# Another order of up and down products in the 256-column passes of the second mixture of experts

## The chip, the cores and the metric

The kernel runs on one core of a Trainium2 chip. The metric is device time in microseconds (us) of one execution; lower is better.

## What is computed

Three stages follow each other: an attention masked by clusters (2 x 8 heads, 768 positions, head size 64), a first mixture of experts with a maximum over three products, and the second mixture of experts, in which the change lies. Cut to that stage:

```
x: 1536 x 512, w_gate: 512 x 8, w1: 8 x 512 x 1024, w2: 8 x 1024 x 512
P = exp(x @ w_gate - max)
8 times: P /= row sums; P /= column sums; P *= N / E
for e in range(8):
    h = max(x @ w1[e], 0)
    out += P[:, e:e+1] * (h @ w2[e])
```

## The kernel before, in words

All products are float32: each operand is split into a high and a low part, and `three` (lines 705 to 709) issues three matmuls for one product of 128 rows.

The second mixture works in 32 **units**, n = 0 to 31: one expert and one pair of 128-row slices of its 1024 hidden columns. Each unit has two **passes** over the tokens (`PASSES`): a **wide** one (i = 0) of 512 columns and a **narrow** one (i = 1) of 256 columns. Tokens are halved, so that a Strassen-like scheme of seven products stands for eight.

`up_products` yields after each of its seven products; an **up block** is six matmuls of 512 or 256 columns. In the order of the code they are, with the accumulator bank they write: U1 (x), U2 (y), U3 (x again, added), U4 (y again, added), U5 (z), U6 (w), U7 (z again, added). What reads them in between:

- after U1, ScalarE copies bank x to `a` (L1062). U3 adds to bank x, so it waits for that copy.
- after U2, VectorE adds y and `a` into `u2` (L1065). U4 adds to bank y, so it waits for that add.
- after U3, a rectifier (L1045 on ScalarE, L1046 on VectorE) makes the first hidden tile, h11; after U4, VectorE adds y and `a` into `u3` (L1071).
- U5, U6 and U7 are followed by one VectorE add or subtraction each (c22 L1074, c21 L1078, c12 L1082) and a rectifier each. U7 waits for the read of bank z by c22.

`down` yields after each **down block** (D): six matmuls of 512 columns into one of four banks `l`, then one VectorE instruction that scales and accumulates into `acc` (L1106; L1101 for the first expert, L1104 besides for its last pair). Down blocks work on the pass before: a narrow pass runs the eight down blocks D1 to D8 of its unit's wide pass, and a wide pass runs the four of the previous unit's narrow pass.

The order in which a pass issues up and down blocks is a string in the table `WAYS` (L1116), `u` for up and `d` for down, and nothing else reorders it: each engine runs its instructions in program order.

```
WAYS = {(0, 0): "uuuu", (0, 1): "uudddudddudd", 0: "uuduuduudud", 1: "uuddudududududd"}
```

Between the blocks, counted by up blocks, the loop also issues the weight conversions of the next unit (ScalarE, L863 and L873, GpSimd, L864 and L874), the fetch of further weights (SyncE, after the fourth up block of a narrow pass), and in units 1 and 2 the steps of the gate (the repeated normalisation of P): after the second, fourth and sixth up block of a pass a small matmul `cs` (L1018) on TensorE and a chain of eight small VectorE instructions (L1010 to L1025), which ends in `prob` (L1015) and which the next `cs` waits for.

Of the kernel before, what the change touches and what calls it, by code (L numbers as in the profile page):

```python
# [137 lines left out]
def moe_kernel(ctx: ExitStack, tc: tile.TileContext, qk, nat, cen, wt, w123, wout, wgate, w1, w2, out):  # L138
# [974 lines left out]
    gate = gates()  # L1113
    later = iter(())

    WAYS = {(0, 0): "uuuu", (0, 1): "uudddudddudd", 0: "uuduuduudud", 1: "uuddudududududd"}  # L1116
    for n in range(len(seq)):
        for i in range(2):
            if i == 0:
# [8 lines left out]
            k = 0  # L1128
            for step in WAYS[(0, i) if n == 0 else i]:
                if step == "d":  # L1130
# [69 lines left out]
```

## Time and profile before

| | |
|---|---|
| three runs, us | 1484.22, 1485.67, 1486.05 (median 1485.67) |
| profiled execution, us | 1484.61, of which span 1482.8 |
| TensorE busy | 1446.4 us, 98% of the span |
| VectorE, ScalarE, GpSimd busy | 964.1, 542.1 and 701.8 us (65%, 37%, 47%) |
| second mixture, narrow passes of units 1 to 31 | from 524.28 us to the end |

The page has the busy times, the span in 40 slices, the chain of work that ended last, and the costliest groups. A matmul's end in it is modelled, and matmuls overlap, so the distance between the starts of neighbouring matmuls, rather than the printed duration, tells how long one keeps TensorE. In the second mixture the sequence repeats with a period of 31.00 us per unit from unit 3 on.

### The profile page before, as it was taken

The numbers are of one execution on the slowest core, as the hardware profiler recorded it, in microseconds if no ns is written. First come the engines' busy times: TensorE is split into PE (matmuls) and PEld (weight loads), VectorE is DVE, ScalarE is ACT, GpSimd is POOL, SyncE is SP. The second block draws the span as 40 slices with busy tenths as digits, with TensorE's granted clock in tenths as the row PEclk, the third lists the DMA queues.
The fourth block names the chain that finished last, engine by engine and source line by source line (L and its number), as shares of the span: only waits on it lengthen the run. The fifth ranks groups of instructions, "written<-read, shape, count | busy, mean of one in ns | idle before, by whom it ended". The sixth has DMA issues, their size and how long they took to land.

```text
span 1482.8 us, 20473 instructions
## 1 busy us (share of the span) xinstructions
PE 1446.4 (98%) x7712; PEld 1247.1 (84%) x7712; DVE 964.1 (65%) x1686; ACT 542.1 (37%) x1159; POOL 701.8 (47%) x789
## 2 busy tenths in 40 slices
PE   5999998899999999999999999999999999999998
PEld 4999998788887888888888888888888888888887
DVE  5999888745555686765665655656556665566655
ACT  4888878422223522222222222222223222222221
POOL 5899998755654733343333333333333333333330
PEclk9999999999999999999999999999999999999999
DMA  6664631212121100111000110001100011000102
GB/s 176 174 162 130 154 82 47 69 43 71 54 64 42 56 29 29 30 46 39 29 29 29 44 43 29 29 30 43 43 29 29 29 44 43 29 29 29 44 15 86
DMA packets 32147, 83.44 MB, mean 56 GB/s; under 512 B 4560, under 2 KB 9904, under 8 KB 32048
## 3 DMA queue, kind: packets, MB, share of 16 engines
q1 hardware_dynamic: 32048, 82.13, 19.1%
q8 instruction: 60, 0.98, 0.3%
q14 instruction: 39, 0.32, 0.1%
HBM read 65.55 MB, written 3.19 MB: 46 GB/s over the span
## 4 chain that ended last, share of the span: by engine, by line
PE 84%; DVE 6%; POOL 6%; issue 1%; ACT 1%; DMA 1%; SPq 0%; POOLq 0%; ACTq 0%; DVEq 0%
PE l L707 11%; PE l L708 11%; PE l L709 11%; PE m L707 3%; PE m L709 3%; PE m L708 3%; PE z L709 3%; PE z L708 3%; PE z L707 3%; PE y L709 3%; PE x L709 3%; PE y L708 3%; PE x L708 3%; PE y L707 3%; PE x L707 3%; PE y L510 2%
## 5 line engine op out<-in xcount | busy, mean ns | idle before, releaser
L1106 DVE SCALAR_TENSOR_TENSOR acc<-l,prob,acc 128x512 f32<-128x512 f32 x336 | 251.6, 749 | 126.4 <-PE l L709 123.2
L707 PE MATMUL l<-w,h 128*128 128x512 f32 x768 | 302.2, 393 | 0.0
L708 PE MATMUL l<-w,h 128*128 128x512 f32 x768 | 301.1, 392 | 0.0
L709 PE MATMUL l<-w,h 128*128 128x512 f32 x768 | 298.8, 389 | 0.0
L1045 ACT ACTIVATE h<-c 128x512 fp32r<-128x512 f32 (+1 forms) x186 | 97.6, 525 | 368.8 <-DVE c L1074 190.6
L864 POOL TENSOR_TENSOR wop_t<-ts,wop_t 128x256 fp32r<-128x256 f32 x124 | 91.8, 751 | 245.3 <-ACT wop_t L863 245.3
L864 POOL TENSOR_TENSOR wop_b<-wraw,wop_b 128x256 fp32r<-128x256 f32 x97 | 79.3, 818 | 266.6 <-ACT wop_b L863 266.6
L1046 DVE SCALAR_TENSOR_TENSOR h<-c,h 128x512 fp32r<-128x512 f32 (+1 forms) x186 | 112.6, 605 | 110.0 <-ACT h L1045 110.0
L709 PEld LDWEIGHTS l<-w,h 128*128 128x128 f32 x768 | 144.3, 188 | 31.5
L707 PEld LDWEIGHTS l<-w,h 128*128 128x128 f32 x768 | 145.0, 189 | 24.5
L708 PEld LDWEIGHTS l<-w,h 128*128 128x128 f32 x768 | 145.0, 189 | 22.7
L874 POOL TENSOR_TENSOR w<-wraw,w 128x512 fp32r<-128x512 f32 x64 | 83.2, 1301 | 96.3 <-ACT w L873 96.3
L463 DVE TENSOR_SCALAR_CACHE_REDUCE e<-s 128x768 f32<-128x768 f32 x96 | 92.6, 964 | 17.8 <-PE s L452 17.1
L1045 ACT ACTIVATE h<-x 128x512 fp32r<-128x512 f32 (+1 forms) x62 | 30.4, 491 | 188.2 <-PE x L709 188.2
L471 ACT ACTIVATE e<-e,nm 128x768 f32<-128x768 f32 x96 | 90.0, 937 | 16.3 <-DVE e L463 15.8
L510 PE MATMUL y<-at,v 128*128 128x256 f32 x576 | 91.1, 293 | 3.2 <-DVE x L527 2.0
L510 PEld LDWEIGHTS y<-at,v 128*128 128x128 f32 x576 | 79.5, 192 | 6.2 <-POOL at L239 1.8
L707 PE MATMUL m<-x,mhi 128*128 128x512 f32 x216 | 84.0, 389 | 0.0
L708 PE MATMUL m<-x,mlo 128*128 128x512 f32 x216 | 84.0, 389 | 0.0
L709 PE MATMUL m<-x,mhi 128*128 128x512 f32 x216 | 84.0, 389 | 0.0
L709 PE MATMUL x<-x,wop_b 128*128 128x512 f32 (+1 forms) x248 | 83.3, 336 | 0.0
L709 PE MATMUL y<-s,wop_t 128*128 128x512 f32 (+1 forms) x248 | 83.3, 336 | 0.0
(203 smaller groups left out, 3304.7 us busy)
## 6 DMA issues: line engine op xcount, KB each, us to landing
wraw<-in_w SPq DMA_DIRECT2D x64, 512.0 KB
mraw<-in_w SPq DMA_DIRECT2D x18, 512.0 KB
nat<-in_nat SPq DMA_DIRECT2D x16, 384.0 KB
raw<-in_qk SPq DMA_DIRECT2D x16, 384.0 KB
natv<-in_nat SPq DMA_DIRECT2D x16, 192.0 KB
r<-row SPq DMA_DIRECT2D x16, 192.0 KB
mraw<-in_wout SPq DMA_DIRECT2D x8, 384.0 KB
out<-acc SPq DMA_DIRECT2D x12, 256.0 KB
```

The source lines that it names most:

```text
L463: lambda e: nc.vector.tensor_scalar(ex(), scores(), -SCALE, None, op0=ALU.mult, op1=ALU.min, accum_out=nm()),
L471: lambda e: nc.scalar.activation(ex(), ex(), AF.Exp, bias=nm(), scale=-1.0, accum_out=sm()[:, n]),
L510: nc.tensor.matmul(y(), v()[:, k], at()[:, l, :, k // 3, k % 3 * P : (k % 3 + 1) * P], start=n == 0, stop=n == 2 * NQ - 1)
L707: nc.tensor.matmul(ps, whi, xlo, start=first, stop=False, skip_group_check=more)
L708: nc.tensor.matmul(ps, wlo, xhi, start=False, stop=False, skip_group_check=more)
L709: nc.tensor.matmul(ps, whi, xhi, start=False, stop=last, skip_group_check=more)
L864: nc.gpsimd.tensor_sub(w[:, 1], src[key], f32(w[:, 0]))
L874: nc.gpsimd.tensor_sub(w[:, 1], raw[:, j], f32(w[:, 0]))
L1045: nc.scalar.activation(h[:, :, 0], z, AF.Relu)
L1046: nc.vector.scalar_tensor_tensor(h[:, :, 1], z, 0.0, f32(h[:, :, 0]), op0=ALU.max, op1=ALU.subtract)
L1106: nc.vector.scalar_tensor_tensor(acc[tt], l2, prob[:, tt, e : e + 1], acc[tt], op0=ALU.mult, op1=ALU.add)
```

## The change

One string of the table changes, that of the narrow pass of units 1 to 31: four up blocks, four down, one up, three down, two up, one down. The same seven up and eight down blocks are issued, with the same instructions behind each.

```diff
-    WAYS = {(0, 0): "uuuu", (0, 1): "uudddudddudd", 0: "uuduuduudud", 1: "uuddudududududd"}
+    WAYS = {(0, 0): "uuuu", (0, 1): "uudddudddudd", 0: "uuduuduudud", 1: "uuuudddduddduud"}
```

TensorE, narrow pass of unit 8, before: the first of the six matmuls of each block (`x8`, `y8` are the banks of U1 to U4, `l2` those of the down blocks; `[waits ...]` names the engines whose semaphores it waits for).

```order
L707 MATMUL x8_1_7963<-x2_0_5044,wop8_b11_7604 128x256 [waits PE_49]
...
L707 MATMUL y8_1_7964<-s2_0_5327,wop8_t2_7631 128x256
...
L707 MATMUL l2_8_1_0_0_7993<-w2_8_0_7787,h8_0_21_7931 128x512 [waits Activation_49,Pool_49]
...
L707 MATMUL l2_8_1_0_1_8001<-w2_8_0_7787,h8_0_21_7931 128x512
...
L707 MATMUL x8_1_7963<-x2_2_5234,wop8_b21_7662 128x256 [waits Activation_49]
...
L707 MATMUL l2_8_1_0_2_8021<-w2_8_0_7787,h8_0_21_7931 128x512 [waits DVE_49]
...
L707 MATMUL y8_1_7964<-s3_0_5328,wop8_t3_7708 128x256 [waits DVE_49]
...
L707 MATMUL l2_8_1_0_3_8041<-w2_8_0_7787,h8_0_21_7931 128x512
```

The same place now:

```order
L707 MATMUL x8_1_7963<-x2_0_5044,wop8_b11_7604 128x256 [waits PE_49]
...
L707 MATMUL y8_1_7964<-s2_0_5327,wop8_t2_7631 128x256
...
L707 MATMUL x8_1_7963<-x2_2_5234,wop8_b21_7662 128x256 [waits Activation_49]
...
L707 MATMUL y8_1_7964<-s3_0_5328,wop8_t3_7708 128x256 [waits DVE_49]
...
L707 MATMUL l2_8_1_0_0_8017<-w2_8_0_7787,h8_0_21_7931 128x512 [waits Pool_49]
...
L707 MATMUL l2_8_1_0_1_8025<-w2_8_0_7787,h8_0_21_7931 128x512
...
L707 MATMUL l2_8_1_0_2_8033<-w2_8_0_7787,h8_0_21_7931 128x512
...
L707 MATMUL l2_8_1_0_3_8041<-w2_8_0_7787,h8_0_21_7931 128x512
```

U3 and U4, which wait for ScalarE and for VectorE, stand directly behind U1 and U2; before, two down blocks stood ahead of U3 and one more ahead of U4.

VectorE at the same place, before: from the last rectifier of the wide pass on.

```order
L1046 SCALAR_TENSOR_TENSOR h8_0_12_7952<-c12_8_0_7856,h8_0_12_7952 128x2x256 [waits Activation_49]
L1106 SCALAR_TENSOR_TENSOR acc5_5467<-l2_7_0_512_1_7955,prob_77,acc5_5467 128x512 [waits PE_49]
L1065 TENSOR_TENSOR u2_8_1_7968<-y8_1_7964,a8_1_7967 128x256 [waits PE_49,Activation_49]
L1106 SCALAR_TENSOR_TENSOR acc6_5468<-l2_8_1_0_0_7993,prob_77,acc6_5468 128x512 [waits PE_49]
L1106 SCALAR_TENSOR_TENSOR acc7_5469<-l2_8_1_0_1_8001,prob_77,acc7_5469 128x512 [waits PE_49]
L1046 SCALAR_TENSOR_TENSOR h8_1_11_8015<-x8_1_7963,h8_1_11_8015 128x256 [waits Activation_49]
L1106 SCALAR_TENSOR_TENSOR acc8_5470<-l2_8_1_0_2_8021,prob_77,acc8_5470 128x512 [waits PE_49]
L1071 TENSOR_TENSOR u3_8_1_7969<-y8_1_7964,a8_1_7967 128x256 [waits PE_49]
```

And now:

```order
L1046 SCALAR_TENSOR_TENSOR h8_0_12_7952<-c12_8_0_7856,h8_0_12_7952 128x2x256 [waits Activation_49]
L1106 SCALAR_TENSOR_TENSOR acc5_5467<-l2_7_0_512_1_7955,prob_77,acc5_5467 128x512 [waits PE_49]
L1065 TENSOR_TENSOR u2_8_1_7968<-y8_1_7964,a8_1_7967 128x256 [waits PE_49,Activation_49]
L1046 SCALAR_TENSOR_TENSOR h8_1_11_7999<-x8_1_7963,h8_1_11_7999 128x256 [waits Activation_49]
L1071 TENSOR_TENSOR u3_8_1_7969<-y8_1_7964,a8_1_7967 128x256 [waits PE_49]
L1106 SCALAR_TENSOR_TENSOR acc6_5468<-l2_8_1_0_0_8017,prob_77,acc6_5468 128x512 [waits PE_49]
L1106 SCALAR_TENSOR_TENSOR acc7_5469<-l2_8_1_0_1_8025,prob_77,acc7_5469 128x512 [waits PE_49]
L1106 SCALAR_TENSOR_TENSOR acc8_5470<-l2_8_1_0_2_8033,prob_77,acc8_5470 128x512 [waits PE_49]
```

The add into `u2` keeps its place: behind the last rectifier and the last accumulation of the wide pass. Behind it the rectifier and the add into `u3` moved ahead of the four accumulations.

TensorE in the narrow pass of unit 1, where the gate's column sums `cs1` and `cs2` stand among the blocks, before:

```order
L707 MATMUL y1_1_5944<-s2_1_5515,wop1_t2_5589 128x256
...
L1018 MATMUL cs1_5916<-prob_77,ones_71 128x96 [waits DVE_49]
...
L707 MATMUL l2_1_1_0_0_5989<-w2_1_0_5722,h1_0_21_5895 128x512 [waits Activation_49]
...
L707 MATMUL l2_1_1_0_1_5997<-w2_1_0_5722,h1_0_21_5895 128x512
...
L707 MATMUL x1_1_5943<-x2_2_5234,wop1_b21_5616 128x256 [waits Activation_49]
...
L707 MATMUL l2_1_1_0_2_6017<-w2_1_0_5722,h1_0_21_5895 128x512
...
L707 MATMUL y1_1_5944<-s3_0_5328,wop1_t3_5635 128x256 [waits DVE_49]
...
L1018 MATMUL cs2_5988<-prob_77,ones_71 128x96 [waits DVE_49,PE_49]
```

And now:

```order
L707 MATMUL y1_1_5944<-s2_1_5515,wop1_t2_5589 128x256
...
L1018 MATMUL cs1_5916<-prob_77,ones_71 128x96 [waits DVE_49]
...
L707 MATMUL x1_1_5943<-x2_2_5234,wop1_b21_5616 128x256 [waits Activation_49]
...
L707 MATMUL y1_1_5944<-s3_0_5328,wop1_t3_5635 128x256 [waits DVE_49]
...
L1018 MATMUL cs2_5988<-prob_77,ones_71 128x96 [waits DVE_49,PE_49]
...
L707 MATMUL l2_1_1_0_0_6029<-w2_1_0_5722,h1_0_21_5895 128x512
```

Between the two column sums only two up blocks are left; three down blocks moved behind the second.

## Rows read from the trace of the kernel before

**Rows 1.** The page: the busy line of its section 1, the clock line of its section 2 (tenths of full speed, 40 equal slices) and the chain's shares by engine.

```profile
PE 1446.4 (98%) x7712; PEld 1247.1 (84%) x7712; DVE 964.1 (65%) x1686; ACT 542.1 (37%) x1159; POOL 701.8 (47%) x789
...
PEclk9999999999999999999999999999999999999999
...
PE 84%; DVE 6%; POOL 6%; issue 1%; ACT 1%; DMA 1%; SPq 0%; POOLq 0%; ACTq 0%; DVEq 0%
```

**Rows 2.** Timeline of TensorE in unit 17 (columns: start us, duration us, engine, line, operation, tiles, shapes). The last matmul of the wide pass's fifth up block, then the first matmul of blocks U1, U2, D1, D2 and U3 of the narrow pass, and of the first block of unit 18's wide pass.

```profile
1017.79 0.39 PE L709 MATMUL z<-x,wop_t 128*128 128x512 f32 x1
...
1023.46 0.28 PE L707 MATMUL x<-x,wop_b 128*128 128x256 f32 x1
...
1024.17 0.28 PE L707 MATMUL y<-s,wop_t 128*128 128x256 f32 x1
...
1024.89 0.40 PE L707 MATMUL l<-w,h 128*128 128x512 f32 x1
...
1026.28 0.39 PE L707 MATMUL l<-w,h 128*128 128x512 f32 x1
...
1027.64 0.28 PE L707 MATMUL x<-x,wop_b 128*128 128x256 f32 x1
...
1039.50 0.39 PE L707 MATMUL x<-x,wop_b 128*128 128x512 f32 x1
```

**Rows 3.** Timeline of VectorE in unit 17, all its instructions from the fifth up block of the wide pass to the add of L1065 in the narrow pass; in brackets the idle time before an instruction and what ended it.

```profile
1018.22 0.69 DVE L1074 TENSOR_TENSOR c<-z,u 128x512 f32<-128x512 f32 x1 [0.61 <-PE z L709]
1019.61 0.69 DVE L1046 SCALAR_TENSOR_TENSOR h<-c,h 128x512 fp32r<-128x512 f32 x1 [0.70 <-ACT h L1045]
1020.22 0.68 DVE L1078 TENSOR_TENSOR c<-u,w 128x512 f32<-128x512 f32 x1
1021.60 0.69 DVE L1046 SCALAR_TENSOR_TENSOR h<-c,h 128x512 fp32r<-128x512 f32 x1 [0.70 <-ACT h L1045]
1022.21 0.75 DVE L1106 SCALAR_TENSOR_TENSOR acc<-l,prob,acc 128x512 f32<-128x512 f32 x1
1022.87 0.68 DVE L1082 TENSOR_TENSOR c<-z,u 128x512 f32<-128x512 f32 x1
1024.25 0.69 DVE L1046 SCALAR_TENSOR_TENSOR h<-c,h 128x512 fp32r<-128x512 f32 x1 [0.70 <-ACT h L1045]
1024.86 0.74 DVE L1106 SCALAR_TENSOR_TENSOR acc<-l,prob,acc 128x512 f32<-128x512 f32 x1
1025.52 0.41 DVE L1065 TENSOR_TENSOR u<-y,a 128x256 f32<-128x256 f32 x1
```

**Rows 4.** Timeline of ScalarE in unit 17: its last rectifier of the wide pass and the copy of L1062 in the narrow pass.

```profile
1023.59 0.63 ACT L1045 ACTIVATE h<-c 128x512 fp32r<-128x512 f32 x1 [1.72 <-DVE c L1082]
1024.43 0.38 ACT L1062 COPY a<-x 128x256 f32<-128x256 f32 x1 [0.21 <-PE x L709]
```

**Rows 5.** Timelines of TensorE and VectorE: U1's first matmul and the add of L1065 of the narrow pass, in unit 5 and in unit 31.

```profile
651.46 0.28 PE L707 MATMUL x<-x,wop_b 128*128 128x256 f32 x1
...
1457.46 0.28 PE L707 MATMUL x<-x,wop_b 128*128 128x256 f32 x1
...
653.52 0.41 DVE L1065 TENSOR_TENSOR u<-y,a 128x256 f32<-128x256 f32 x1
...
1459.52 0.41 DVE L1065 TENSOR_TENSOR u<-y,a 128x256 f32<-128x256 f32 x1
```

**Rows 6.** Timelines in the attention part: VectorE's accumulator read, the weight load and the matmuls of a score block that waited for it (start 139.28), and the same pair of matmuls where nothing was waited for (start 69.03).

```profile
139.14 0.08 DVE L463 DVE_READ_ACCUMULATOR e<-s 128x1 f32 x1
...
139.28 0.30 PEld L449 LDWEIGHTS s<-opmb,opsb 128*128 128x128 f32 x2 [0.64 <-DVE e L463]
...
139.28 0.62 PE L449 MATMUL s<-opmb,opsb 128*128 128x384 f32 x2 [0.40 <-DVE e L463]
...
139.74 0.52 PE L452 MATMUL s<-opm 80*128 80x384 f32 x2
...
69.03 0.51 PE L449 MATMUL s<-opmb,opsb 128*128 128x384 f32 x2
...
69.38 0.51 PE L452 MATMUL s<-opm 80*128 80x384 f32 x2
```

**Rows 7.** Timelines of the narrow passes of units 1, 2 and 4. Unit 1: the first matmul behind the gate's column sum, ScalarE's copy of L1062, VectorE's add of L1065 and the last step of the gate's chain that the next column sum reads; unit 2: the first matmul behind the column sum, and the add; unit 4: U1's first matmul, and the add.

```profile
526.02 0.49 PE L707 MATMUL l<-w,h 128*128 128x512 f32 x1
...
526.81 0.38 ACT L1062 COPY a<-x 128x256 f32<-128x256 f32 x1
...
527.22 0.42 DVE L1065 TENSOR_TENSOR u<-y,a 128x256 f32<-128x256 f32 x1
...
529.92 0.26 DVE L1015 TENSOR_TENSOR prob<-prob,rr 128x96 f32<-128x96 f32 x1
...
559.79 0.48 PE L707 MATMUL l<-w,h 128*128 128x512 f32 x1
...
561.40 0.41 DVE L1065 TENSOR_TENSOR u<-y,a 128x256 f32<-128x256 f32 x1
...
620.46 0.28 PE L707 MATMUL x<-x,wop_b 128*128 128x256 f32 x1
...
623.97 0.41 DVE L1065 TENSOR_TENSOR u<-y,a 128x256 f32<-128x256 f32 x1
```

**Rows 8.** Timeline of VectorE: its first add of unit 17's wide pass, with the idle time before it, and from the end of the narrow pass the half-width rectifier behind U6 and the last accumulation.

```profile
1011.49 0.69 DVE L1065 TENSOR_TENSOR u<-y,a 128x512 f32<-128x512 f32 x1 [2.04 <-PE y L709]
...
1035.76 0.43 DVE L1046 SCALAR_TENSOR_TENSOR h<-c,h 128x256 fp32r<-128x256 f32 x1 [0.48 <-ACT h L1045]
...
1039.70 0.75 DVE L1106 SCALAR_TENSOR_TENSOR acc<-l,prob,acc 128x512 f32<-128x512 f32 x1 [0.45 <-PE l L709]
```


## The prediction

> **What bounds the kernel now.** I read the page first, then the chain, then the timelines of one unit. TensorE is busy for 98% of the span, its clock line stands at 9 in every slice, and the chain that ended last runs on it for 84% [rows 1]. So each microsecond that TensorE stands still is lost, and each one it works less is won; the other engines matter only where TensorE waits for them. In unit 17 it waits for nobody: U1, U2 and D1 start 0.71 and 0.72 us apart, D2 starts 1.39 us behind D1 and U3 1.36 us behind D2, and the whole narrow pass takes 1039.50 - 1023.46 = 16.04 us [rows 2]. That is just what such steps add up to: an up block costs 0.71 us behind a down block and 0.72 behind an up block, a down block 1.39 behind an up block and 1.36 behind a down block.
>
> VectorE, though only 65% busy, is late at this very place. From the fifth up block of the wide pass it never waits for TensorE again: the first add of the row starts 0.04 us after that block's last matmul ends (1017.79 + 0.39 = 1018.18) [rows 2, 3], and then rectifiers, adds and two accumulations follow in a row, with pauses for ScalarE's half of a rectifier only (0.70 us each), until the add of L1065 ends at 1025.93 [rows 3]. It ends 2.47 us after U1 began. In units 5 and 31 it is the same: 653.52 + 0.41 - 651.46 and 1459.52 + 0.41 - 1457.46 are both 2.47 [rows 5]. Nothing suffers from it now, because U4, which waits for that add, comes three down blocks later.
>
> **The change, part by part.** No instruction is added or removed, and each is issued behind the same up block as before, the weight conversions and SyncE's fetch too.
>
> *Fewer switches: a gain.* The narrow pass had six down blocks behind an up block and has three now; it had one up block behind an up block and has four. By the steps above [rows 2] that is 3 x (1.39 - 1.36) - 3 x (0.72 - 0.71) = 0.06 us per pass, 1.9 us over 31. The starts are printed to 0.01 us, so the bounds are 0 and 0.12 us per pass, 0 to 3.7 us.
>
> *U3 behind U2: almost nothing.* U3 is due 1.43 us after U1 (1024.89) and waits for ScalarE's copy, which ends at 1024.81 [rows 2, 4]. The release takes a little: in the attention part the accumulator read ended at 139.22 and the waiting matmul began at 139.28, 0.06 us later [rows 6]. So the copy is in time by 0.02 us; but the weight load of the waiting matmul began only at the release too, and the next matmul came 0.46 us later, against 0.35 where nothing was waited for [rows 6]. A wait thus costs up to 0.11 us of weight load that otherwise lies beside other matmuls. U3 may lose that, yet it only moves U3 within the wait that follows.
>
> *U4 behind U3: a new wait in every unit.* U4 is due 0.71 us behind U3, at 2.14 us after U1. The add that it waits for ends at 2.47. That add stands behind the same VectorE instructions as before, and their row is tied to the wide pass, which does not change; so it will end at 2.47 again. With 0.06 us for the release and 0.11 us for the weight load, U4 works from 2.64: 0.50 us lost. I take this for 28 units (3 and 5 to 31): 14.0 us. The bounds are 0.39 (the weight load costs nothing), 10.9 us, and 0.61 (it costs twice), 17.1 us.
>
> The Trainium skill ("TensorE: Matmul & The Clock Gate", section on the array's architecture) says that TensorE's queue "can pull LDWEIGHTS ahead of in-flight MATMULs". If it did so past a waiting matmul, the lower bound would hold, 10.9 us in place of 14.0. The rows of the attention part speak against it, as the load itself began at the release [rows 6]; I go by the rows.
>
> *Unit 4: more.* VectorE is held up by the extra scaling of the first expert's last pair, and the add ends at 623.97 + 0.41 = 624.38, 3.92 us after U1 [rows 7]. U4 loses 3.92 + 0.17 - 2.14 = 1.95 us.
>
> *Units 1 and 2: the gate.* In unit 1, U3 now follows the column sum and is due at 526.02; the copy ends at 527.19, so U3 loses 1.34 us and starts at 527.36. U4 follows at 528.07, since the add ended at 527.64. The second column sum is then due at 528.79, but it needs `prob`, which is ready at 530.18 [rows 7]: with 0.06 and 0.11 us, 1.56 us are lost. Together 2.90 us; a bank that the column sum may share with the first up block could hold it up by one more VectorE instruction, so 2.6 to 3.4. In unit 2 U3 is due at 559.79 and U4 at 560.50; the add ends at 561.81 [rows 7], so 561.98 - 560.50 = 1.48 us are lost (1.3 to 1.7).
>
> *What is late next.* After U4 VectorE has two short instructions and then four accumulations of 0.75 us, one per down block of 1.36 us or more, so it catches up. At the end of the pass U6, U7 and D8 follow each other. Behind U6 VectorE has four half-width instructions of about 0.42 us, two pauses of 0.48 us for ScalarE and one accumulation of 0.75 us [rows 3, 8], 3.4 us, and it begins some 0.2 us after TensorE has gone on (the last matmul's tail, 0.28 us long at steps of 0.12); TensorE needs 0.72 + 1.39 = 2.1 us to the end of the pass. So VectorE ends about 1.5 us behind the pass, where its last accumulation ends 0.95 us behind it now (1039.70 + 0.75 against 1039.50) [rows 2, 8]. It was idle for 2.04 us ahead of its first add of a wide pass [rows 8]; about 1.5 us of that cover are left, and the next wide pass starts its row in time.
>
> *Sum.* 14.0 + 1.95 + 1.48 + 2.90 = 20.3 us lost, 1.9 won: 18.4 us slower. Against the profiled execution that is 1484.61 + 18.4 = 1503.0 us; the median of the three runs stands 1.06 us above it, which would give 1504.1. I predict 1503.5 us, between the two. The bounds give 16.6 - 3.7 = 12.9 us, 1497.5, and 24.3 us with no gain, 1508.9, or 1510 from the median.
>
> **The rivals.**
>
> *The weight load is hidden (1499.3).* As above, with the lower bound at each wait: 16.6 - 1.9 = 14.7 us. For it: in the unhindered stream a load does start beside the matmul before it. Against it: the load that began at the release [rows 6].
>
> *Slower by more (about 1512).* VectorE's lateness at the end of the narrow pass eats the 1.5 us of cover and is carried into the next wide pass, where its own second down blocks or U4 then wait. Each 0.3 us that this adds per unit is worth 31 x 0.3 = 9.3 us. For it: U6 and U7 now stand side by side, with both their rectifiers behind them. Against it: the idle 2.04 us [rows 8], and the row that decides starts with a wait for TensorE, 0.61 us long [rows 3].
>
> *Faster (1482.7).* The add of L1065 is read off too late, or gets done earlier, so that U4 finds it done; then only the gain of 1.9 us is left. It decides at 1.97 us after U1: ended by then, the add costs nothing. The nearest thing that could bring it there is the 0.66 us of the accumulation ahead of it [rows 3], if that were issued behind the add; in the program it still stands ahead. That matmul ends are modelled could shift TensorE's times against VectorE's, but the 0.04 us between a matmul's end and the add that waited for it [rows 2, 3] leave no room for 0.5.
>
> *No difference.* The change would not do what it says, or waits and gain would cancel; the order of the rows has moved as written, and 14 against 1.9 us do not cancel.
>
> **How the numbers follow.** My forecast has a chance of 0.65, the hidden weight load 0.20, slower by more 0.08, faster 0.04, no difference 0.03. A measurement of this kernel can tell about 0.2%, 3 us, from no change. All slower cases lie far beyond that: slower 0.93, same 0.03, faster 0.04. The range of 1497 to 1510 us takes in the bounds of the sum and the hidden weight load, and leaves out the carried lateness and the two cases without loss.
>
> **What would show it.** In the changed kernel TensorE should stand still once per narrow pass, ahead of the first matmul of U4, with the add of L1065 as releaser, for about 0.4 us as the view of waits counts it, some 30 times; the period per unit should be about 31.43 us in place of 31.00. Down blocks should start 1.39 us ahead of the next one three times per pass. Wide passes should show no wait. In unit 1 U3 should wait for ScalarE's copy and the second column sum for `prob`. The prediction is wrong if U4 does not wait, if the add ends well ahead of or behind 2.47 us after U1, or if TensorE waits anywhere else in a unit.

## The result, and the profile after

The changed kernel takes 1504.9 us (median of 4 runs, 1503.89 to 1506.35) against 1485.15 us: ratio 1.0136, 95% interval 1.0123 to 1.0148. It is 1.4% slower, about 20 us, and lies 1.4 us above the forecast of 1503.5. The profiled execution has a span of 1503.3 us against 1482.8.

From the page: the busy line of TensorE and the chain by engine.

```profile
PE 1456.9 (97%) x7712; PEld 1252.3 (83%) x7712; DVE 969.3 (64%) x1686; ACT 542.4 (36%) x1159; POOL 705.1 (47%) x789
...
PE 80%; POOL 7%; DVE 6%; ACT 4%; issue 2%; DMA 1%; SPq 0%; ACTq 0%; POOLq 0%; DVEq 0%
```

TensorE works the same matmuls as in [rows 1], but for 97% of a longer span. ScalarE's share of the chain went from 1% to 4%, which is to be read with care (below). What TensorE waited for in the second mixture is in the view of waits (us in total, times, longest); the same view of before has one wait there, 0.9 us for a column sum.

```profile
PE y L707 <- DVE u L1065: 5.9, 28, 1.5
PE cs L1018 <- DVE prob L1015: 1.7, 1, 1.7
PE cs L1018 <- DVE c L1082: 1.5, 2, 1.0
PE x L707 <- ACT a L1062: 1.5, 2, 1.0
```

The first line is the forecast one: 28 times for the add of L1065, in units 4 to 31. The others are the gate's, in units 1 and 2. This view counts a matmul's modelled tail as busy, so its sums are lower bounds of what was lost. The timeline of TensorE (and of its weight load, PEld) in unit 17 tells that, from start to start.

```profile
1037.94 0.28 PE L707 MATMUL x<-x,wop_b 128*128 128x256 f32 x1
...
1038.65 0.28 PE L707 MATMUL y<-s,wop_t 128*128 128x256 f32 x1
...
1039.37 0.35 PE L707 MATMUL x<-x,wop_b 128*128 128x256 f32 x1
...
1039.55 0.28 PE L708 MATMUL x<-x,wop_b 128*128 128x256 f32 x1
...
1040.47 0.38 PE L707 MATMUL y<-s,wop_t 128*128 128x256 f32 x1 [0.17 <-DVE u L1065]
...
1040.70 0.28 PE L708 MATMUL y<-s,wop_t 128*128 128x256 f32 x1
...
1041.29 0.40 PE L707 MATMUL l<-w,h 128*128 128x512 f32 x1
...
1040.47 0.19 PEld L707 LDWEIGHTS y<-s,wop_t 128*128 128x128 f32 x1 [0.37 <-DVE u L1065]
...
1054.38 0.39 PE L707 MATMUL x<-x,wop_b 128*128 128x512 f32 x1
```

U4 starts at 1040.47, 2.53 us after U1, and its second matmul 0.23 us later, its next ones 0.12 us apart. Its weight load began at the release too. D1 starts 3.35 us after U1 where 2.86 had been due: 0.49 us. U3's second matmul comes 0.18 us behind its first, not 0.12: its load, which waits for the copy, lost 0.06 us. The pass takes 16.44 us (before 16.04 [rows 2]). VectorE in the same place:

```profile
1039.34 0.75 DVE L1106 SCALAR_TENSOR_TENSOR acc<-l,prob,acc 128x512 f32<-128x512 f32 x1
1040.00 0.41 DVE L1065 TENSOR_TENSOR u<-y,a 128x256 f32<-128x256 f32 x1
1040.76 0.42 DVE L1046 SCALAR_TENSOR_TENSOR h<-x,h 128x256 fp32r<-128x256 f32 x1 [0.34 <-ACT h L1045]
1041.48 0.42 DVE L1071 TENSOR_TENSOR u<-y,a 128x256 f32<-128x256 f32 x1 [0.30 <-PE y L709]
```

The accumulation still stands ahead of the add, the add ends at 1040.41, 2.47 us after U1, to 0.01 us as before the change [rows 3, 5], and the first matmul of U4 starts 0.06 us behind it.

The chain that ended last tells this place otherwise (start, us, what):

```profile
1039.28 0.71 ACT wop_t L863 x2
...
1040.00 0.43 DVE u L1065
...
1040.47 0.38 PE y L707
```

It puts the add down to ScalarE's two weight conversions of L863, the second of which ended just before it, and not to VectorE's accumulation. These conversions and the copy ahead of them make most of ScalarE's larger share. The run that moves the accumulation tells the two apart (below): there the add starts while the second conversion still runs, so it does not wait for it.

Set beside each other, from the first matmul of U1 in unit 1 to that in unit 31 (before 524.28 to 1457.46, after 523.81 to 1477.54, thus 20.55 us more):

| | before, us | after, us | more, us | forecast, us |
|---|---|---|---|---|
| unit 1 | 32.73 | 38.17 | 5.44 | 2.84 |
| unit 2 | 32.45 | 34.89 | 2.44 | 1.42 |
| unit 3 | 31.00 | 31.27 | 0.27 | 0.44 |
| unit 4 | 31.00 | 32.85 | 1.85 | 1.89 |
| units 5 to 30, each | 31.00 | 31.41 | 0.41 | 0.44 |

(forecast: the wait less 0.06 us for the switches.) In unit 3 the accumulation ahead of the add is the shorter one of L1101 (0.69 us), the add ends 2.35 us after U1, and so the unit loses less than the others. Units 1 and 2 lost 7.9 us where 4.3 were forecast. The timeline of unit 1 shows where, TensorE first, then VectorE's chain and GpSimd:

```profile
525.30 0.46 PE L1018 MATMUL cs<-prob,ones 128*128 128x96 f32 x2
...
526.77 0.39 PE L707 MATMUL x<-x,wop_b 128*128 128x256 f32 x1 [1.01 <-ACT a L1062]
...
527.59 0.28 PE L707 MATMUL y<-s,wop_t 128*128 128x256 f32 x1
...
530.21 0.43 PE L1018 MATMUL cs<-prob,ones 128*128 128x96 f32 x2 [1.75 <-DVE prob L1015]
...
530.42 0.48 PE L707 MATMUL l<-w,h 128*128 128x512 f32 x1
...
537.60 0.28 PE L707 MATMUL z<-x,wop_t 128*128 128x256 f32 x1
...
528.98 0.32 DVE L1012 TENSOR_SCALAR rse<-rs 128x12 f32<-128x12 f32 x1
...
529.59 0.47 DVE L1015 TENSOR_TENSOR prob<-prob,rr 128x96 f32<-128x96 f32 x1
...
527.10 2.17 POOL L864 TENSOR_TENSOR wop_t<-ts,wop_t 128x256 fp32r<-128x256 f32 x3 [4.06 <-ACT wop_t L863]
...
529.22 0.72 POOL L864 TENSOR_TENSOR wop_b<-wraw,wop_b 128x256 fp32r<-128x256 f32 x1
```

U3 behind the column sum starts at 526.77; due 0.25 us after the column sum, it lost 1.22 us, and 0.11 more to its weight load. The second column sum, due at 528.30, starts at 530.21, 1.91 us late in place of 1.56: `prob` is ready at 530.06, 6.25 us after U1 in place of 5.90 [rows 7]. Two steps of its chain are longer: the last took 0.47 us here and 0.26 there [rows 7], the one of L1012 0.32 here and 0.17 there, as the timeline of before shows.

```profile
529.45 0.17 DVE L1012 TENSOR_SCALAR rse<-rs 128x12 f32<-128x12 f32 x1
```

With the up blocks the weight conversions moved together as well, and GpSimd now runs without a pause to 529.94, beside the chain; before, it rested from 529.02 to 530.55, while these two steps ran. Then four down blocks take from 530.42 to 537.60, 7.18 us, where the first costs 1.47 behind a column sum and the others 1.36, 5.55 in all. The view of busy time by stretch tells why (columns: length, PE, PEld, DVE, ACT, POOL busy with instructions, granted clock, DMA share, GB/s).

```profile
528.00:530.50 2.50, 0.75 (x7) 0.58 (x6) 2.33 (x8) 0.87 (x3) 1.94 (x3) 1.00 0.00 0
530.50:533.00 2.50, 2.50 (x11) 2.00 (x10) 2.26 (x10) 0.00 (x0) 0.00 (x0) 0.74 0.65 192
533.00:535.50 2.50, 2.50 (x8) 1.98 (x7) 0.99 (x2) 0.00 (x0) 0.00 (x0) 0.58 0.04 18
535.50:538.00 2.50, 2.50 (x14) 2.09 (x13) 0.93 (x3) 0.00 (x0) 0.00 (x0) 1.00 0.00 0
```

From 530.50 to 535.50 the granted clock is 0.74 and 0.58 of full speed on average, which is some 3.4 us at 1.2 GHz in place of 2.4. It fell behind the two waits, the second of which stands in the stretch before (0.75 us of work in 2.5). That cost 1.6 us. In unit 2 it fell behind two waits (column sum and U3), just before U4 waited too.

### The profile page after: what moved, and what is told of

Same layout as the page of the kernel before. It is cut to its first block, busy times and chain, and to the rows that moved or that the text cites. A ratio compares the mean times of both kernels' runs of the same rounds, so it can differ in the third digit from the quotient of the medians.

```text
span 1503.3 us, 20443 instructions
## 1 busy us (share of the span) xinstructions
PE 1456.9 (97%) x7712; PEld 1252.3 (83%) x7712; DVE 969.3 (64%) x1686; ACT 542.4 (36%) x1159; POOL 705.1 (47%) x789
## 4 chain that ended last, share of the span: by engine, by line
PE 80%; POOL 7%; DVE 6%; ACT 4%; issue 2%; DMA 1%; SPq 0%; ACTq 0%; POOLq 0%; DVEq 0%
PE l L707 11%; PE l L708 11%; PE l L709 11%; PE m L708 3%; PE m L709 3%; PE m L707 3%; PE z L707 3%; PE z L709 3%; PE z L708 3%; PE y L707 3%; PE y L708 2%; PE x L709 2%; PE y L709 2%; PE x L707 2%; PE x L708 2%
## 5 line engine op out<-in xcount | busy, mean ns | idle before, releaser
L1046 DVE SCALAR_TENSOR_TENSOR h<-c,h 128x512 fp32r<-128x512 f32 (+1 forms) x186 | 117.7, 633 | 110.1 <-ACT h L1045 110.1
L707 PE MATMUL y<-s,wop_t 128*128 128x512 f32 (+1 forms) x248 | 86.6, 349 | 5.9 <-DVE u L1065 5.9
L708 PE MATMUL y<-s,wop_t 128*128 128x512 f32 (+1 forms) x248 | 83.5, 337 | 0.0
```

The lines of the kernel that those rows point to most:

```text
L707: nc.tensor.matmul(ps, whi, xlo, start=first, stop=False, skip_group_check=more)
L708: nc.tensor.matmul(ps, wlo, xhi, start=False, stop=False, skip_group_check=more)
L1046: nc.vector.scalar_tensor_tensor(h[:, :, 1], z, 0.0, f32(h[:, :, 0]), op0=ALU.max, op1=ALU.subtract)
```

## The experiments

Theory A: U4's wait for the add makes the loss, with the gate's waits and the clock behind them in units 1 and 2. Theory B: grouping four up and four down blocks costs by itself, in every unit alike. Theory C, of the clock alone: it falls by chance, or at the first wait.

**Where the loss lies: early units apart.** Units 1 and 2 keep the old order.

```diff
-            for step in WAYS[(0, i) if n == 0 else i]:
+            for step in "uuddudududududd" if i == 1 and 0 < n < PAIRS - 1 else WAYS[(0, i) if n == 0 else i]:
```

> Units 1 and 2 keep the old narrow order, units 3 to 31 have the new one. Theory A (each unit loses about 0.41 us net because U4 waits for VectorE's add; units 1 and 2, with the gate, lose 5.4 and 2.4 us besides): 1504.9 - 7.9 = 1497.0 us, period of a late unit still 31.40 us. Theory B (grouping four up and four down blocks costs the same in each of the 31 units, 20 us / 31 = 0.65 us): 1504.9 - 1.3 = 1503.6 us.

Measured: 1496.95 us, ratio 1.0085 (1.0068 to 1.0102). Units 1 and 2 take 32.72 and 32.46 us as before the change, unit 20 31.42 us. The other way round, with the two strings exchanged, so that units 1 and 2 alone have the new order:

> Only units 1 and 2 have the new narrow order, units 3 to 31 the old one. Theory A: the 7.9 us that the two units lost in the changed kernel come back alone: 1484.6 + 7.9 = 1492.5 us, if TensorE's clock falls in both again; about 2.7 us less for falls that do not recur. Theory B (the same loss in each unit): 1484.6 + 1.3 = 1485.9 us.

Measured: 1492.11 us, ratio 1.0044 (1.0029 to 1.0059); unit 1 takes 38.17 us, unit 2 34.84 us, all others 31.00. The two parts add up (12.4 and 7.9 us), and B as it stands is out: two units of 31 carry 40% of the loss. Whether grouping costs something in the late units is for the next runs.

**VectorE's row: the accumulation behind the add.** `accumulate` is the accumulation of L1096 to L1108 as a function; it is put off in a list `held`, which starts empty.

```diff
+                if i == 1 and r == 0 and t == c // P - 1 and PAIRS - 1 <= n < len(seq) - 1:
+                    held.append(accumulate)
+                else:
+                    accumulate()
...
                     next(ups)
+                    if i == 1 and k == 1:
+                        while held:
+                            held.pop(0)()
```

> New order in all units, but the last accumulation of a wide pass is issued on VectorE behind the add of L1065 (for the narrow passes of units 4 to 31). Theory A: the add ends some 0.66 us earlier, about 1.81 us after U1, U4 does not wait, the period falls from 31.40 to about 30.91 us, unit 4 loses about 1.6 us less: 1504.9 - 13.2 - 1.6 = 1490.1 us. Theory B (the grouping itself costs, whatever VectorE does): period 31.40, 1504.9 us.

Measured: ratio 1.0060 (1.0043 to 1.0077), three executions at 1492.1 to 1495.5 us; a fourth took 7675.05 us, at a granted clock of 0.178 on average, and is left out. The period of a late unit is 31.07 us. VectorE, ScalarE and TensorE in unit 20:

```profile
1128.22 0.42 DVE L1065 TENSOR_TENSOR u<-y,a 128x256 f32<-128x256 f32 x1 [0.22 <-ACT wop_t L863]
...
1128.56 0.74 DVE L1107 SCALAR_TENSOR_TENSOR acc<-l,prob,acc 128x512 f32<-128x512 f32 x1
...
1127.75 0.80 ACT L863 CAST wop_t<-ts 128x256 fp32r<-128x256 f32 x2
...
1126.52 0.28 PE L707 MATMUL x<-x,wop_b 128*128 128x256 f32 x1
...
1127.83 0.28 PE L709 MATMUL y<-s,wop_t 128*128 128x256 f32 x1
...
1128.73 0.36 PE L707 MATMUL y<-s,wop_t 128*128 128x256 f32 x1
...
1128.92 0.28 PE L708 MATMUL y<-s,wop_t 128*128 128x256 f32 x1
```

The add now stands ahead of the accumulation and ends at 1128.64, 2.12 us after U1, and U4 starts 2.21 us after U1, its second matmul 0.19 us later. So 0.34 of the 0.41 us are gone and A holds; but the add did not end at 1.81. With VectorE free, U2's own end sets it: U2's last matmul started at 1127.83 and lasts 0.28 us, and the add starts 0.11 us behind its end. The bracket names a conversion of ScalarE, the first of two; but the add of a wide pass, which waits for TensorE, starts 0.11 us behind U2's end as well (1011.49 [rows 8] behind 1011.38 in the kernel before). The second conversion ran on to 1128.55, so it holds up no add. U2, add and U4 make a chain that one up block between them does not quite cover; the weight load is still late.

**The dose: one more VectorE instruction ahead of the add.**

```diff
+        if i == 1:
+            nc.vector.tensor_tensor(dose, ident, ident, op=ALU.mult)
         nc.vector.tensor_add(u2, y, a)
```

> The change, with one more VectorE instruction (a product of 128 x 128 elements into a scratch tile that nobody reads, some 0.2 to 0.3 us) ahead of the add of L1065 in each narrow pass. Theory A (VectorE's row ahead of that add sets U4's start): the add ends later by the instruction's whole time, the period grows by the same, 31.40 to about 31.65 us, the kernel by some 7 to 9 us to about 1512. Theory B (the loss lies in TensorE's order): VectorE has time to spare at 64% busy, the period stays at 31.40 us.

Measured: 1520.2 us, ratio 1.0233 (1.0216 to 1.0250). Unit 20:

```profile
1144.43 0.55 DVE L1067 TENSOR_TENSOR dose<-ident 128x128 f32<-128x128 f32 x1
...
1144.90 0.41 DVE L1068 TENSOR_TENSOR u<-y,a 128x256 f32<-128x256 f32 x1
...
1142.37 0.28 PE L707 MATMUL x<-x,wop_b 128*128 128x256 f32 x1
...
1145.36 0.38 PE L707 MATMUL y<-s,wop_t 128*128 128x256 f32 x1 [0.63 <-DVE u L1068]
```

The instruction took 0.55 us, twice what was expected; the add ends at 1145.31, 2.94 us after U1 in place of 2.47, and U4 starts 0.05 us behind it. The period went from 31.41 to 31.87 us: 0.47 us of lateness, 0.46 us of time. VectorE is 65% busy, and at this place it has nothing to spare. In unit 4 of this run TensorE stood still once, for 2.18 us, and the granted clock fell behind that one wait:

```profile
633.86 0.38 PE L707 MATMUL y<-s,wop_t 128*128 128x256 f32 x1 [2.18 <-DVE u L1068]
...
635.00:637.50 2.50, 2.50 (x8) 1.92 (x7) 0.65 (x2) 0.28 (x1) 0.74 (x1) 0.51 0.12 33
```

So unit 4 takes 35.19 us in place of 32.85. In the changed kernel it waits 1.45 us at the same place, and the clock stays.

**Grouping without the wait.** First, one down block ahead of U4.

```diff
-    WAYS = {(0, 0): "uuuu", (0, 1): "uudddudddudd", 0: "uuduuduudud", 1: "uuuudddduddduud"}
+    WAYS = {(0, 0): "uuuu", (0, 1): "uudddudddudd", 0: "uuduuduudud", 1: "uuududdduddduud"}
```

> Narrow order uuududddudddduud cut to u u u d u d d d u d d d u u d: one down block now stands ahead of U4, the rest is grouped as in the change. Theory A: U4 is due 3.53 us after U1, the add ends at 2.47, no wait; period about 30.94 us (two switches fewer than before the change); units 1 and 2 still lose some 3 us together: about 1486.5 us. Theory B (grouping costs): three quarters of the loss stay, about 1500 us.

Measured: 1490.24 us (1487.08 to 1492.04), ratio 1.0038 (1.0025 to 1.0051). From unit 5 on the period is 30.99 to 31.02 us and TensorE waits for no add: B's three quarters are not there. The gain of 0.06 us is not there either, as U3 directly behind U2 gives 0.05 us back to its weight load. Units 1 and 2 take 35.01 and 33.16 us, 3.0 us more than before; the profiled execution, at 1487.08, is the fastest of the five. The others took some 3 us more at a granted clock of 0.997 and 0.998 on average, where the profiled one had 1.000; where it fell in them no trace shows.

Second, three switches and a down block between U2 and U3, from unit 3 on, units 1 and 2 as before the change.

```diff
-    WAYS = {(0, 0): "uuuu", (0, 1): "uudddudddudd", 0: "uuduuduudud", 1: "uuuudddduddduud"}
+    WAYS = {(0, 0): "uuuu", (0, 1): "uudddudddudd", 0: "uuduuduudud", 1: "uuduudddduudddu"}
...
-            for step in WAYS[(0, i) if n == 0 else i]:
+            for step in "uuddudududududd" if i == 1 and 0 < n < PAIRS - 1 else WAYS[(0, i) if n == 0 else i]:
```

> Units 1 and 2 keep the old narrow order; units 3 to 31 run u u d u u d d d d u u d d d u: as few down blocks behind up blocks as the change (three), but a down block stands between U2 and U3, and U4 is due 3.5 us after U1. Theory A (the change's loss is the wait alone, its grouping gains a little): no wait for the add but in unit 4 (about 0.55 us), period about 30.94 us in place of 31.00, about 1.1 us faster than before the change, ratio 0.999. Theory B (grouping costs by itself): slower than before by several us.

Measured: 1484.62 us against 1484.16, ratio 0.9997 (0.9988 to 1.0007): no difference. The period is 30.96 us from unit 5 on, so the grouping gains 0.04 us per unit; units 3 and 4 give back 0.17 and 0.50 us. The last up block now stands ahead of the next wide pass, which pays a switch there. What is left, some 0.4 us, is below what can be measured: no version here beats the kernel before.

**The clock.** In narrow passes the gate takes no step behind U4, so that unit 1 has no second column sum there.

```diff
-                    if n == 0 and i == 0 and k < 2 or 0 < n < PAIRS and k % 2 == 1:
+                    if n == 0 and i == 0 and k < 2 or 0 < n < PAIRS and k % 2 == 1 and not (i == 1 and k == 3):
```

> New order, but in narrow passes the gate takes no step behind the fourth up block, so that unit 1 has no column sum between U4 and D1. Theory A (TensorE's clock falls to half in unit 1 because it waits twice in a row, 1.3 and 1.9 us, at U3 and at the second column sum): no second wait, the granted clock stays at 1.00 in unit 1, which takes about 3.5 us less (38.17 to about 34.7 us). Theory C (the first wait, or the stage, is enough): the granted clock still falls to about 0.5 for some 3.7 us, and unit 1 takes only about 1.9 us less.

Measured: 1501.12 us in one run. Unit 1 takes 34.04 us in place of 38.17. U3 still waits there for the copy (1.01 us in the view of waits), and the granted clock behind it:

```profile
530.50:533.00 2.50, 2.50 (x13) 2.07 (x12) 1.70 (x3) 0.00 (x0) 0.00 (x0) 1.00 0.64 210
533.00:535.50 2.50, 2.50 (x16) 2.17 (x15) 1.48 (x3) 0.81 (x2) 0.00 (x0) 1.00 0.00 0
```

It stays at 1.00. So the first wait alone did not bring the clock down in unit 1; with the second it fell. The version with one down block ahead of U4 agrees: there the second column sum waits 0.17 us only, and the clock stays in unit 1. In unit 2 of this run, where TensorE waits 1.34 us for VectorE ahead of the column sum and 0.46 us ahead of U3, it did fall, to 0.59 from 562.50 to 565.00. And the changed kernel once more, without an edit, for its trace:

> The changed kernel once more, for its trace. Theory A (the clock falls in units 1 and 2 because of the waits there): the granted clock falls in units 1 and 2 again and nowhere else in the second mixture. Theory C (the falls come at random): it falls at other places, or not.

Measured: 1507.67 us in one run; units 1 and 2 take 38.17 and 34.90 us again.

```profile
535.00:537.50 2.50, 2.50 (x8) 1.92 (x7) 1.01 (x3) 0.00 (x0) 0.00 (x0) 0.50 0.10 41
...
567.50:570.00 2.50, 2.01 (x10) 1.67 (x9) 2.21 (x6) 1.66 (x6) 1.44 (x2) 0.67 0.00 0
```

The clock falls in both units again, and nowhere else in the second mixture; it did so too where units 1 and 2 alone had the new order. In the attention stage, which no edit touches, it falls in some executions and not in others, and the kernel before had such a fall at 211 us. That moves whole runs by some microseconds and is why the periods of the units say more than the medians.

## Why the prediction was right

The forecast was slower by 18.4 us, with one wait per unit as the cause; 20.5 us were measured in the profiled executions, inside the range, and the sum's places are the right ones. That the time came within 1.4 us is in part luck: units 1 and 2 lost 3.6 us more than forecast, and units 3 to 30 together 1.1 us less.

- *U4's wait.* Right to 0.03 us per unit (0.41 net, forecast 0.44), but for unit 3 (0.27), whose add ends earlier: the add ended 2.47 us after U1, as forecast from rows that the change leaves alone, the release took 0.06 us, and 0.49 us were lost where 0.50 were forecast. The undone accumulation, the dose and the down block put ahead of U4 each moved the loss the way the step said. Only the sign named for it, about 0.4 us in the view of waits, was off: the view shows 0.17, because it counts the tail of U3's last matmul as busy.
- *The weight load.* The rows of the attention part were the better guide: U4's load began at the release, and U4's block took 0.81 us in place of 0.72. So the rival of 1499.3 us falls. The pulling ahead of which the Trainium skill speaks ("TensorE: Matmul & The Clock Gate", section on the array's architecture) did not reach past a waiting matmul: that load starts at 1040.47, with the matmul and not before it, and its own row names the add as what it waited for.
- *U3.* In time by 0.02 us, as said, and 0.06 us of its weight load lost within the other wait.
- *The gain from fewer switches.* 0.07 to 0.1 us in the changed kernel, when 0.49 and the rest are set against the period; 0.04 us in the version without waits. The forecast 0.06 stands within what starts printed to 0.01 us can tell.
- *Unit 4.* 1.85 us, forecast 1.89.
- *Units 1 and 2.* The mechanism was right, the size was not: 7.9 us, forecast 4.3, above the upper bounds of both terms (3.4 and 1.7 us). Three things were missing. The clock: TensorE ran at half speed behind the waits, about 1.6 us in unit 1 and 1.1 us in unit 2 (from 566.93 to 574.27 it took 7.34 us for U4 and four down blocks, in unit 17 6.27). In the run with the accumulation moved, whose unit 2 has the same instructions and no fall, unit 2 lost 1.39 us, where 1.42 were forecast. The chain to `prob`, 0.35 us longer beside a busy GpSimd: I counted that the conversions stay behind the same up blocks, not that these had moved together. And the first column sum of unit 2's wide pass, which waited 0.6 us for VectorE, late from unit 1: a wait in a place where the prediction saw none.
- *The cover at the end of the pass* held: no wait in a wide pass from unit 3 on. The rival that carried lateness on falls, and so does the faster one.

What stays open is what exactly lets the clock fall. In unit 1 five traces with the second wait (the change twice, units 1 and 2 alone, the accumulation moved, the dose) show the fall, and two with the first wait alone or nearly so (the gate moved, one down block) do not. In unit 4 a single wait of 2.18 us had it behind it, and one of 1.45 us had not. In unit 2 the clock fell in four traces (the change twice, units 1 and 2 alone, the gate moved) and not in those of the accumulation, the dose and the one down block, though all of these but the one with the moved gate wait the same 1.04 and 0.46 us ahead of U3. That GpSimd is what slows the steps of the chain was read from traces and not tried.

## What to carry to other kernels

A saturated TensorE with no wait in its profile can still stand a few tenths of a microsecond ahead of a result: before blocks are moved, take for each accumulation into a used bank the end of the last read of that bank, and compare it with the new start, whichever engine seems idle on average. The blocks between a product and its second part are the cover, and the row of instructions ahead of that read on its engine sets how much is needed. Where waits come to stand close together, or one grows long, leave room in the range for a clock that falls behind them.

## What the runs showed of the hardware

- The granted clock fell to half for about 3.4 us after TensorE had waited 1.2 and 1.9 us in close succession in unit 1, and not after the first of these waits alone. In the run with the dose it fell after one wait of 2.18 us.
- A VectorE product of 128 x 128 elements took 0.55 us (median of 31) in the narrow pass, in unit 20 with GpSimd at work from 1144.09 on. It took 0.28 us in units 1 and 31, where GpSimd rested, but 0.29 us in unit 2 too, where GpSimd worked; the slowest took 0.806. The Trainium skill ("GPSIMD Engine Reference", section on specifications) names contention of GpSimd with VectorE instructions that have two SBUF inputs, as this one has; all but unit 2 fits that, and no run tried it.
- The wait of an accumulating matmul sits on its weight load: U4's load and U4's first matmul both start at 1040.47, and the second matmul follows 0.23 us later instead of 0.12.
